# Attention and routed experts on one core: the hand-made list order is extended over the whole program, and the rows of a token tile are turned by transposes into one bank

## The chip, the cores and the metric

One core of a Trainium2 chip runs the whole program. The metric is device microseconds of one execution, median of three. The engines are PE (TensorE matmuls; PEld are its weight loads), DVE (VectorE), ACT (ScalarE), POOL (GpSimd) and SP (SyncE, which issues most DMAs). Each of them works through a queue in the order in which the program wrote it.

## The reference, cut to what matters

Two batches of eight heads attend over 576 positions with a learned bias on the distance. The 1152 output rows of 512 numbers then go to one of eight experts each, the best by a linear gate; an expert takes at most 288 rows, in order of the tokens.

```python
scores = scale * q @ k.T + bias          # bias: a two-layer net of log distances
attn = exp(scores - max) / (sum + 1e-09)
x = (attn @ v) as [1152, 512]
logits = x @ w_gate;  expert = argmax(logits);  gate = softmax(logits)[expert]
row i is kept if fewer than 288 earlier rows chose its expert
h = relu(x_e @ w1[e]);  y = h @ w2[e];  out[i] = gate * y   (0 if not kept)
```

## The kernel before, in words

**Attention.** There are 40 units: 10 token tiles (five of each batch, four of 128 rows and one of 64) by four pairs of heads. Unit n passes through these tasks, named as in the list that orders them:

- ("S", n): scores on PE into the PSUM pool "s" (two buffers of two banks each, which a full unit fills both).
- ("L", n, i): on DVE, L218, bias added and the row extreme taken; the bias tile bt has come back from a round trip through DRAM.
- ("X", n, i): the exponential on ACT, L225.
- ("R", n) and ("T", n): transposes on PE, L233. R puts the last 64 columns into spare columns of the score banks of unit n+2; T fills pool "tt".
- ("C", n, i): copies out of PSUM, on ACT or DVE. ("C", n, 2), L265, copies what R wrote.
- ("V", n): the product with v on PE, L288, into the one bank "av".

The bias itself is made in 36 blocks in the first 100 us: hidden rows ("H"), a product on PE ("M"), a copy to the tile bo ("E", L160 and L162), a store to DRAM ("D", L168).

**A token tile** (after four units). ("A"): av is copied to xT. ("BM"), tile_b, L319: xT is multiplied by a constant idwg of identity and gate weights side by side, 144 columns for each of four blocks of 128, into the banks "pt" and "av". ("BC"), tile_c: the DVE divides by the sums, first the logits (L355), then the rows x (L361), in four steps of the list. ("BD"): x is stored to DRAM.

**Routing.** The tiles form three groups. ("GA"), ("GB"), ("GC") turn a group's logits into a key for each row. ("P", z), pick, chooses the expert of stream z with most rows; ("MT", z, j), match (L442), and ("FE", z), fetch (L452 and the indirect loads of L460), bring its rows into X.

**The plain stream.** Three blocks of expert work run without branches: z = 0 and 1 for up to 288 rows, z = 2 for 96. Each has eight chunks of weights (load "WL", L639; high part "WH" on ACT or DVE; low part "WO" on DVE or POOL), turned rows ("XM", L654), the first layer in eight parts of 12 matmuls ("FM", L674, then "FH" and "FL" out of the bank) and the second layer of 4 x 24 matmuls (L707). Block 2 has its own forms (L746, L752, L723). Further experts sit behind branches and do not run here.

**The order.** Until the last attention unit every instruction is placed by place_tasks. It holds a clock for each engine, takes the tasks that can start within 0.3 us of the earliest, and writes out the one of lowest rank:

```python
first = min(b[0] for b in best)
at, rank, name, e, chosen = min((b for b in best if b[0] <= first + 0.3), key=lambda b: (b[1], b[0]))
```

Ranks are in units: L has n + 0.1, group 1 has 35.4 to 35.6, P(1) 35.7, P(2) and MT(1) 36, BC of a tile its last unit + 4.3. A task may take a bank, and the next user of it waits until the tasks named with it are done. In this part the expert blocks have the single bank "pt", which the row work of a tile, the routing and the fetches use as well. The DVE instructions for one score reduction, two picks and eight matches are thus in one fixed row.

After the list comes a second part, from tile_a(1, 4) on. The banks of the attention are given back, seven banks "fps" are opened (rest_pools), and the rest of block 0 (step(0, 10) onward: its second layer), the last tile, block 1 and block 2 are written in order for PE, while the framework orders the other engines.

Of the kernel before, what the change touches and what calls it, by code (L numbers as in the profile page):

```python
# [28 lines left out]
def kernel(ctx: ExitStack, tc: tile.TileContext, cap, ins, out):  # L29
# [15 lines left out]
    att = ExitStack()  # L45
    big = att.enter_context(tc.tile_pool(name="big", bufs=2, space=PSUM))
# [6 lines left out]
    kraw_p = att.enter_context(tc.tile_pool(name="kraw", bufs=8))  # L53
    qp = att.enter_context(tc.tile_pool(name="qp", bufs=3))
    vp = att.enter_context(tc.tile_pool(name="vp", bufs=4))
    ep = att.enter_context(tc.tile_pool(name="ep", bufs=4))
    atp = att.enter_context(tc.tile_pool(name="atp", bufs=4))
    vrp = att.enter_context(tc.tile_pool(name="vrp", bufs=4))
    bp = att.enter_context(tc.tile_pool(name="bp", bufs=4))
# [233 lines left out]
    xTs = {}  # L293
    bpt = {}
# [13 lines left out]
    def tile_b(b, t):  # L308

        n = 128 if t < 4 else 64  # L310
        xT = xTs.pop((b, t))

        if "ps" in F:
            ps = [ffn_psum() for _ in range(2)]
        else:
            ps = [pst.tile([128, 512], F32, name="pt"), psm.tile([128, 4, 128], F32, name="av").rearrange("p a c -> p (a c)")]
# [3 lines left out]
        if t == 4:  # L320
            nc.tensor.matmul(ps[1][:64, 256:260], lhsT=ident[:, 64:128], rhs=sums_t[b, t][:, 0:4], start=True, stop=True)
        bpt[b, t] = ps

    def tile_c(b, t):
# [11 lines left out]
        x = xp.tile([128, DM], F32, name="x")  # L336
        sums = sums_t.pop((b, t))
        inv = sm.tile([128, H], F32, name="inv")
        if t < 4:
            nc.vector.tensor_scalar(inv, sums, 1e-9, None, op0=ALU.add)  # L340
        else:
            iv = inv.rearrange("p (a r) -> p r a", r=2)
            nc.vector.tensor_scalar(iv[:64, 0], sums[:64, 0:4], 1e-9, None, op0=ALU.add)
            nc.vector.tensor_scalar(iv[:64, 1], ps[1][:64, 256:260], 1e-9, None, op0=ALU.add)
        nc.vector.reciprocal(inv[:n], inv[:n])
        yield
        for what in range(2):
            if what:
                yield
            for z, (k0, k1) in enumerate(((0, 3), (3, 4))):  # L350
                v = ps[z][:n, 0:144 * (k1 - k0)].rearrange("p (k c) -> p k c", c=144)
                h0, h1 = 2 * k0, 2 * k1
                iv = inv[:n, h0:h1].rearrange("p (k r) -> p k r", r=2).unsqueeze(3)
                if what == 0:
                    nc.vector.tensor_tensor(lg[:n, i, h0:h1].rearrange("p (k r) e -> p k r e", r=2),  # L355
                                            v[:, :, 128:144].rearrange("p k (r e) -> p k r e", r=2),
                                            iv.to_broadcast([n, k1 - k0, 2, E]), op=ALU.mult)
                else:
                    if z:
                        yield  # L360
                    nc.vector.tensor_tensor(x[:n, D * h0:D * h1].rearrange("p (k r d) -> p k r d", r=2, d=D),  # L361
                                            v[:, :, 0:128].rearrange("p k (r d) -> p k r d", r=2),
                                            iv.to_broadcast([n, k1 - k0, 2, D]), op=ALU.mult)
        xs[b, t] = x
# [130 lines left out]
    idwg = const.tile([128, 4, 144], F32, name="idwg")  # L495
# [9 lines left out]

    def gate_const():
        nc.vector.tensor_copy(idwg[:, :, 0:128], ident.unsqueeze(1).to_broadcast([128, 4, 128]))
        nc.vector.tensor_copy(idwg[:, :, 128:144], wgt.rearrange("p (k c) -> p k c", k=4))
# [64 lines left out]
    def rest_list():  # L573
# [8 lines left out]
        nc.vector.tensor_tensor(sel8, sel8, bc(need), op=ALU.mult)  # L582
        nc.vector.reduce_sum(lstf[:, 2 * E:2 * E + 1], need, axis=AX.X)
# [3 lines left out]
        nc.vector.reduce_sum(lstf[:, E:2 * E], tmp8, axis=AX.X)  # L587
        nc.vector.tensor_copy(lst[:, 0:2 * E + 1], lstf[:1, 0:2 * E + 1])
# [8 lines left out]
    def ffn_pools():  # L597
# [9 lines left out]
        Y.append(w0.tile([128, DM], F32, name="y0"))  # L607
# [33 lines left out]
    def weights(z, c):  # L641

        weights_load(z, c)
        split_w(RAW[c % len(RAW)], wbuf(z, c), "ad")

    def ffn_psum():
        return F.get("ps", pst).tile([128, 512], F32, name="pt")
# [3 lines left out]
    def x_mm(x, k, nb):  # L651
        px = fps["x", k] = ffn_psum()
# [16 lines left out]
    def l1_mm(f, w):  # L669
        wh, wl = (u.rearrange("p (k c) -> p k c", k=4)[:, :, 128 * (f % 2):128 * (f % 2) + 128] for u in w)  # L670
        ph = fps["h", f] = ffn_psum()
# [16 lines left out]
    def rows_out(z, a, py):  # L688

        y = Y[F["n"] % len(Y)]  # L690
        F["n"] += 1
        nc.scalar.activation(y[:TB], py[:TB], AF.Copy, scale=SLT[z][:, a, 0:1])
        d = nc.gpsimd.indirect_dma_start(  # L693
            out=out, out_offset=bass.IndirectOffsetOnAxis(ap=SLI[z][:, a:a + 1], axis=0), in_=y[:TB], in_offset=None,
# [4 lines left out]
    def layer2(d, ws):  # L699
# [58 lines left out]
    def step(z, i):  # L758

        if i < 2:  # L760
            for k in range(2 * i, 2 * i + 2):
                x_parts(X[0], k, NB)
            if z and i:
                for a in range(NB):
                    layer2_out(0, a)
# [461 lines left out]
```

## Time and profile before

| | us |
|---|---|
| median of three runs | 324.32 (321.94 to 325.65) |
| the profiled execution | 323.12 |
| its span, first to last instruction | 321.3 |
| PE / DVE / ACT / POOL busy | 268.0 / 205.6 / 171.8 / 87.2 |
| mean granted clock of TensorE, as a share of 2.4 GHz | 0.930 |

Busy times of PE are modelled from starts and pipelined ends, so a stretch in which PE is busy can still run at half clock: the granted clock beside it says at which of the two levels. The profiled execution lies 1.8 us above its span and 1.2 us under the median.

### The profile page before, as it was taken

How to read it: one execution, taken by the hardware profiler on the slowest of the kernel's cores; microseconds unless marked ns; L12 is line 12 of the kernel's file. 1: busy time of each engine (PE TensorE's matmuls, PEld its weight loads, DVE VectorE, ACT ScalarE, POOL GpSimd, SP SyncE). 2: the span in 40 equal slices, each digit the busy share in tenths (PEclk: the TensorE clock that was granted, in tenths of full speed). 3: DMA queues.
4: the chain of work that ended last, by engine and by line, in shares of the span. 5: the costliest groups of instructions: out<-in, count | busy, mean ns of one | idle time of the engine just before them, and what ended most of it. 6: DMA issues, size and time to landing. Idle time of an engine off the chain costs nothing. (4 is left out here: it accounts for less than half of the span.)

```text
span 321.3 us, 7361 instructions
## 1 busy us (share of the span) xinstructions
PE 268.0 (83%) x2801; PEld 202.6 (63%) x2801; DVE 205.6 (64%) x568; ACT 171.8 (53%) x401; POOL 87.2 (27%) x83
## 2 busy tenths in 40 slices
PE   2974977898899898988895989998398869999890
PEld 1521535544455686866584768887287869999870
DVE  4894898598578666577773856856832597950110
ACT  4874677697486546655554473554301357841230
POOL 3794496387460200001252100010030120300031
PEclk9999899999999799999958999999755989999997
DMA  6989595884954732998799575200220599300020
GB/s 172 359 251 332 164 372 157 277 317 150 325 225 152 277 125 65 338 288 265 231 310 290 149 257 155 61 35 0 67 86 22 211 338 414 118 2 0 2 75 16
DMA packets 27628, 59.84 MB, mean 186 GB/s; under 512 B 3813, under 2 KB 5349, under 8 KB 27585
## 3 DMA queue, kind: packets, MB, share of 16 engines
q1 hardware_dynamic: 26688, 56.82, 52.5%
q0 software_dynamic: 896, 2.47, 2.7%
q8 instruction: 24, 0.39, 0.5%
q14 instruction: 20, 0.16, 0.1%
HBM read 42.57 MB, written 16.99 MB: 185 GB/s over the span
## 5 line engine op out<-in xcount | busy, mean ns | idle before, releaser
L218 DVE CUSTOM_DVE_ANT_0 ed<-s,bt 128x576 f32<-128x576 f32 x72 | 53.2, 753 | 30.3 <-PE s L233 15.2
L128 POOL TENSOR_SCALAR hid<-c_u,nbv 128x400 f32<-128x400 f32 (+17 forms) x42 | 59.0, 1417 | 29.3 <-PE tt L147 14.5
L225 ACT ACTIVATE ed<-ed,mn 128x576 f32<-128x576 f32 x72 | 55.8, 776 | 15.8 <-DVE mn L218 14.6
L201 PE MATMUL s<-kraw,q 64*128 64x288 f32 x256 | 46.5, 439 | 4.3 <-ACT rt L265 3.1
L288 PE MATMUL av<-at,vt 128*64 128x128 f32 (+1 forms) x576 | 45.4, 291 | 2.4 <-DVE x L361 1.6
L288 PEld LDWEIGHTS av<-at,vt 128*64 128x64 f32 x576 | 35.8, 149 | 9.1 <-issue 2.8
L201 PEld LDWEIGHTS s<-kraw,q 64*128 64x128 f32 x256 | 25.9, 190 | 17.2 <-ACT rt L265 4.6
L130 ACT ACTIVATE hid<-c_u,c_v 128x528 f32<-128x528 f32 (+17 forms) x52 | 31.4, 659 | 7.8 <-PE tt L147 4.1
L233 PE MATMUL tt<-c_ident,ed 64*128 64x64 f32 x576 | 27.9, 237 | 3.3 <-DVE bo L160 1.7
L265 ACT COPY rt<-s 128x64 f32<-128x64 f32 (+1 forms) x68 | 11.2, 212 | 36.0 <-DVE mn L218 27.2
L233 PEld LDWEIGHTS tt<-c_ident,ed 64*128 64x128 f32 x576 | 23.1, 147 | 10.9 <-issue 4.8
L247 ACT COPY at<-tt 128x512 f32<-128x512 f32 x44 | 24.1, 581 | 6.7 <-PE tt L233 3.9
L132 DVE TENSOR_SCALAR hid<-c_u,c_v 128x544 f32<-128x544 f32 (+17 forms) x50 | 25.1, 543 | 0.0
L90 ACT CAST wh<-raw 128x1024 fp32r<-128x1024 f32 x16 | 16.6, 1050 | 14.7 <-PE av L288 7.8
L417 POOL TENSOR_SCALAR tokv<-s 128x5 bf16<-128x5 f32 (+2 forms) x3 | 1.6, 549 | 78.1 <-DVE s L415 70.0
L674 PE MATMUL pt<-xh,wh 128*128 128x288 f32 x64 | 21.2, 332 | 1.5 <-DVE hl L681 1.0
L95 DVE TENSOR_TENSOR wl<-raw,wh 128x1024 fp32r<-128x1024 f32 x16 | 19.5, 1219 | 3.6 <-ACT wh L90 3.4
L147 PE MATMUL pt<-hid,c_w2bd 128*32 128x432 f32 (+12 forms) x152 | 17.1, 512 | 4.9 <-DVE bo L160 4.7
L160 DVE TENSOR_SCALAR bo<-pt,c_rv,corr 128x192 f32<-128x192 f32 (+31 forms) x32 | 17.1, 576 | 5.4 <-DMA bd<-bo 3.4
L674 PE MATMUL pt<-xl,wh 128*128 128x288 f32 x64 | 20.4, 318 | 0.0
L674 PE MATMUL pt<-xh,wl 128*128 128x288 f32 x64 | 20.0, 312 | 0.0
L707 PE MATMUL pt<-hh,wh 128*128 128x288 f32 x64 | 20.0, 312 | 0.0
(176 smaller groups left out, 511.9 us busy)
## 6 DMA issues: line engine op xcount, KB each, us to landing
bt<-bd SPq DMA_DIRECT2D x28, 576.0 KB, 4.9
raw<-in_w_dram SPq DMA_DIRECT2D x24, 512.0 KB, 7.3
bd<-bo SPq DMA_DIRECT2D x36, 295.5 KB, 4.0
vt<-in_v_dram SPq DMA_DIRECT2D x8, 320.0 KB, 5.4
kraw<-in_k_dram SPq DMA_DIRECT2D x8, 288.0 KB, 4.7
bt<-bd SPq DMA_DIRECT2D x8, 288.0 KB, 4.5
out_dram<-y SPq DMA_DIRECT2D x3, 768.0 KB, 8.5
q<-in_q_dram SPq DMA_DIRECT2D x8, 256.0 KB, 6.4
```

The costliest lines, as they stand in the source:

```text
L95: (nc.vector if eng[1] == "d" else nc.gpsimd).tensor_tensor(lo, raw, hi.bitcast(F32), op=ALU.subtract)
L128: nc.gpsimd.tensor_scalar(hid[:, :m], wu[:, :m], nbv[:, w:w + 1], None, op0=ALU.max)
L130: nc.scalar.activation(hid[:, :m], wu[:, :m], AF.Relu, bias=bvw[:, w:w + 1])
L132: nc.vector.tensor_scalar(hid[:, :m], wu[:, :m], bvw[:, w:w + 1], 0.0, op0=ALU.add, op1=ALU.max)
L201: nc.tensor.matmul(ps[i][:, r, :HALF], lhsT=q[p, hp], rhs=k[p, r * HALF:(r + 1) * HALF], start=True, stop=True, tile_position=(64 * i, 0))
L218: nc.vector.tensor_tensor_reduce(out=ed.rearrange("p (r j) -> p r j", r=2), in0=ps[:, :, :HALF], in1=bias.rearrange("p (r j) -> p r j", r= ...
L225: nc.scalar.activation(ed, ed, AF.Exp, scale=-1.0, bias=mns.pop((n, i)), accum_out=total)
L233: nc.tensor.transpose(out[r][:w], ed[p, o:o + w], ident[p, p], tile_position=(64 * r, 0))
L247: nc.scalar.copy(o, v)
L288: nc.tensor.matmul(o, lhsT=lh, rhs=rh, start=(j == 0), stop=(j == 4), tile_position=(0, r))
L674: nc.tensor.matmul(ph[:, :cap], lhsT=u[:, k], rhs=x[:, k], start=(k + z == 0), stop=(k == 3 and z == 2))
L707: nc.tensor.matmul(py[:, :cap], lhsT=w, rhs=hx, start=(f + i == 0), stop=(f == 7 and i == 2))
```

## The change

- The list covers everything up to the last scatter. The second part is gone. Tasks exist for the last tile, group 2, the list of remaining experts, all three blocks and every scatter. PSUM is not handed over; block 1 and block 2 take one bank of any of the pools pt, tt, s and av ("ANY"), so five banks in all. SBUF is handed over by a task ("late") after the last V.
- tile_b is split. tile_l ("BL") makes the logits alone into 64 columns of a bank, with the plain gate weights; tile_c ("BC") becomes one step with one product; tile_b ("BM") turns the rows by four transposes into one bank; tile_x ("BX") scales them with one instruction. The bank "av" is not used by them. idwg and the 0.9 us of its making go.
- The model of the list gets other numbers and rules: a bandwidth of 380 KB/us for loads, no latency between tasks of one engine, shorter times for several tasks. ("C", n, 2) now comes after the score reductions of unit n+2, with which it shares banks.
- At the start, loads of K, Q and V wait in the list for earlier transfers (stores of bias blocks, bias tiles).
- Ranks of P, MT(1), L and the tiles stay, BC's becomes lower by one.

```diff
-    def tile_b(b, t):
+    def tile_l(b, t, w="pt"):
...
+        ps = bpt[b, t] = ffn_psum(w)
+        for k in range(4):
+            nc.tensor.matmul(ps[:n, 16 * k:16 * k + 16], lhsT=xTs[b, t][:, k, :n], rhs=wgt[:, 16 * k:16 * k + 16], start=True, stop=True)
...
+    def tile_b(b, t, w="pt"):
...
         for k in range(4):
-            z, o = divmod(144 * k, 432)
-            nc.tensor.matmul(ps[z][:n, o:o + 144], lhsT=xT[:, k, :n], rhs=idwg[:, k], start=True, stop=True)
...
+            nc.tensor.transpose(ps[:n, 128 * k:128 * k + 128], xT[:, k, :n], ident)
...
+    def tile_x(b, t):
...
+        nc.vector.tensor_tensor(x[:n].rearrange("p (h d) -> p h d", d=D), ps[:n].rearrange("p (h d) -> p h d", d=D),
+                                invs.pop((b, t))[:n].unsqueeze(2).to_broadcast([n, H, D]), op=ALU.mult)
...
-                ready = max([ends[a] for a in after], default=0.0)
+                own = engines if len(engines) == 1 and engines != "s" else None
+                ready = max([begun[a[1]] if a[0] == "then" else ends[a] if begun[a, "on"] != own else begun[a] for a in after], default=0.0)
...
+            if kb:
+                moved = max(moved, at + us[e] + 1.0) + kb / 380.0
+                ends[name] = moved + 1.0
...
-            task(("VL", b, hp), "s", 0.45, (lambda b=b, hp=hp: dma_v(b, hp)), after=[slot(17) if b else slot(hp - 3)],
-                 rank=20.0 * b + hp - 1, takes=[("v", users)])
...
+            task(("VL", b, hp), "s", 0.45, (lambda b=b, hp=hp: dma_v(b, hp)), after=[slot(17) if b else slot(hp - 1) or then("B", 0, 4, 1)],
+                 rank=20.0 * b + hp - 1, takes=[("v", users)], kb=320)
...
-        task(("C", n, 2), "da", {"d": 0.3, "a": 0.5}, (lambda e, n=n: turned_rem(n, e)), after=[("R", n)], rank=n + LAG + 0.3, takes=[("rt", [("V", n)])])
+        task(("C", n, 2), "da", {"d": 0.28, "a": 0.25}, (lambda e, n=n: turned_rem(n, e)),
+             after=[("R", n)] + ([("L", n + LAG, i) for i in two(n + LAG)] if not last else []), rank=n + LAG + 0.3, takes=[("rt", [("V", n)])])
...
+        spare = ("pt",) if i < 8 else ("pt", "s", "tt")
+        task(("BL", b, t), "e", 0.4, (lambda w="pt", b=b, t=t: tile_l(b, t, w)), after=[("A", b, t), "wg"], rank=n + 1.1, takes=[(spare, [("BC", b, t)])])
+        task(("BC", b, t), "d", 0.7, (lambda b=b, t=t: tile_c(b, t)), after=[("BL", b, t)], rank=n + 1.3)
+        task(("BM", b, t), "e", 0.9, (lambda w="pt", b=b, t=t: tile_b(b, t, w)), after=[("BL", b, t)], rank=n + 1.2, takes=[(spare, [("BX", b, t)])])
+        task(("BX", b, t), "d", 0.85, (lambda b=b, t=t: tile_x(b, t)), after=[("BM", b, t), ("BC", b, t)], rank=n + 1.5, takes=[("x", [("BD", b, t)])])
...
+    task("late", "p", 0.6, late_pools, after=[("V", n) for n in range(NU - 4, NU)] + ["pools"], rank=40.0)
...
+            task(("WO", z, c), "pd", {"p": 2.4, "d": 1.16},
+                 (lambda e, z=z, c=c, raw=raw: split_lo(e, *wbuf(z, c), raw())), after=[("WH", z, c)], rank=r + 2.5)
...
+    ANY = ("pt", "tt", "s", "av")
+    for z in range(2):
+        pp = ("pt",) if z == 0 else ANY
+        for k in range(4):
+            task(("XM", z, k), "e", 0.35, (lambda w="pt", k=k: x_mm(X[0], k, NB, w)), after=[("FE", z), ("FM", 0, 7) if z else None, "late" if z else None],
+                 rank=(27.0, 43.5)[z] + 0.1 * k, takes=[(pp, [("XL", z, k)])])
...
+            task(("FM", z, f), "e", 1.65, (lambda w="pt", z=z, f=f: l1_mm(f, wbuf(z, f // 2), w)),
+                 after=[("XL", z, k) for k in range(4)] + [("WO", z, f // 2)], rank=(30.0 + 1.4 * f, 50.0 + f)[z],
+                 takes=[(pp, [("FL", z, f)])])
...
+                task(("Y", z, d, g), "e", 0.82, (lambda w="pt", z=z, d=d, g=g: l2_mm(d, [wbuf(z, c) for c in range(4, 8)], g, w)),
+                     after=[("FL", z, 2 * g + 1), ("FL", z, 2 * g), ("WO", z, 4 + g), ("Y", z, d, g - 1) if g else None],
+                     rank=(44.0, 60.0)[z] + d + 0.2 * g,
+                     takes=[(ANY if (z or d) else ("pt",), [("YC", z, d)])] if g == 0 else [])
```

## Rows read from the trace of the kernel before

**Rows 1.** Busy time of the engines, granted clock and DMA, by stretches

```profile
core 0: us, PE busy (x) PEld busy (x) DVE busy (x) ACT busy (x) POOL busy (x), PEclk, DMA share, GB/s
...
24.60:30.16 5.56, 1.24 (x6) 0.69 (x6) 2.17 (x6) 1.90 (x5) 3.39 (x4) 1.00 1.02 342
30.16:226.15 195.99, 174.13 (x2078) 124.51 (x2078) 142.37 (x403) 118.97 (x305) 53.51 (x47) 0.96 0.63 208
226.15:231.05 4.90, 0.00 (x1) 0.01 (x2) 4.76 (x20) 0.92 (x3) 0.00 (x0) 0.76 0.35 107
231.05:249.40 18.35, 16.56 (x148) 14.43 (x149) 6.23 (x22) 4.01 (x11) 3.47 (x4) 0.51 0.16 48
...
261.60:313.90 52.30, 51.17 (x366) 48.02 (x363) 23.79 (x58) 23.65 (x44) 7.52 (x10) 0.97 0.32 118
```

**Rows 2.** Who PE waited for, 200 to 262 us: total, times, longest

```profile
PE s L233 <- ACT ed L225: 4.9, 1, 4.9
PE pt L404 <- DVE oh L386: 2.7, 1, 2.7
```

**Rows 3.** DVE in order of time, 219 to 230 us: start, duration, idle before

```profile
219.01 0.17 DVE L540 TENSOR_TENSOR kept<-pt,rows 128x8 f32<-128x8 f32 x1 [2.00 <-PE pt L539]
...
220.23 0.75 DVE L218 CUSTOM_DVE_ANT_0 ed<-s,bt 128x576 f32<-128x576 f32 x1
...
226.96 2.46 DVE L442 TENSOR_SCALAR match<-iota,key,base 128x288 bf16<-128x288 f32 x7
229.34 0.74 DVE L218 CUSTOM_DVE_ANT_0 ed<-s,bt 128x576 f32<-128x576 f32 x1
```

**Rows 4.** The chain that ended last, in order of time

```profile
192.40 1.78 PE pt L674 x12
...
241.61 3.19 PE pt L674 x12
```

**Rows 5.** PE in order of time, 206 to 231 us

```profile
206.10 1.00 PE L319 MATMUL pt<-idwg,xT 128*128 128x144 f32 x6
...
224.89 1.00 PE L319 MATMUL pt<-idwg,xT 128*128 128x144 f32 x6 [0.60 <-DVE hl L681]
```

**Rows 6.** DVE in order of time, 24 to 30 us

```profile
24.59 0.76 DVE L218 CUSTOM_DVE_ANT_0 ed<-s,bt 128x576 f32<-128x576 f32 x1 [1.23 <-DMA bt<-bd]
...
29.43 1.08 DVE L160 TENSOR_SCALAR bo<-pt,c_rv,corr 128x96 f32<-128x96 f32 x2 [3.39 <-DMA bd<-bo]
```

**Rows 7.** DMA issues of 0 to 36 us: count, KB each, us to landing

```profile
vt<-in_v_dram SPq DMA_DIRECT2D x4, 320.0 KB, 6.5
```

**Rows 8.** PE in order of time, 271 us: the output of block 0 turned

```profile
270.89 1.47 PE L714 MATMUL pt<-c_ident,yt 128*96 128x128 f32 x12
```

**Rows 9.** DVE in order of time, 231 us: the rows of a tile scaled

```profile
231.40 0.55 DVE L361 TENSOR_TENSOR x<-pt,inv 128x384 f32<-128x384 f32 x1
...
231.94 0.28 DVE L361 TENSOR_TENSOR x<-av,inv 128x128 f32<-128x128 f32 x1
```

**Rows 10.** Who waited for whom, whole span: total, times, longest

```profile
PE s L201 <- ACT rt L265: 3.1, 4, 1.1
```

**Rows 11.** The same, waits of ACT

```profile
ACT rt L265 <- DVE mn L218: 27.2, 17, 4.0
```

**Rows 12.** The same, waits of DVE

```profile
DVE ed L218 <- ACT rt L265: 7.6, 17, 1.0
```

**Rows 13.** PE in order of time, 172 to 175 us: rows of block 0 turned

```profile
172.35 0.30 PE L654 MATMUL pt<-c_ident,xe 96*128 96x96 f32 x1 [2.08 <-DMA xe<-xd,sli]
174.16 0.42 PE L654 MATMUL pt<-c_ident,xe 96*128 96x96 f32 x1 [1.51 <-DMA xe<-xd,sli]
```

**Rows 14.** POOL in order of time, 215 and 261 us

```profile
215.73 0.20 POOL L417 TENSOR_SCALAR tokv<-s 128x3 bf16<-128x3 f32 x1 [31.91 <-DVE s L415]
...
261.29 1.23 POOL L417 TENSOR_SCALAR tokv<-s 128x2 bf16<-128x2 f32 x1 [8.02 <-DVE oh L386]
```

**Rows 15.** DVE in order of time, 261 us

```profile
261.24 1.23 DVE L95 TENSOR_TENSOR wl<-raw,wh 128x1024 fp32r<-128x1024 f32 x1
```

More of the change, by code (lines that the diff above doesn't have):

```diff
@@ L335, in tile_c @@
         lg = glg[g]
[L336 removed]
         sums = sums_t.pop((b, t))
[L338 removed]
+        inv = invs[b, t] = sm.tile([128, H], F32, name="inv")
         if t < 4:
@@ L606, in ffn_pools @@
             F[nm] = w0.tile([128, m, cap], F32R, name=nm)
-        Y.append(w0.tile([128, DM], F32, name="y0"))
+        Y.extend(w0.tile([128, DM], F32, name=f"y{k}") for k in range(3))
+        F["yt"] = w0.tile([128, 4, cap], F32, name="yt")
         F["n"] = 0
@@ L775, in small, with st_hi @@
[L775 to L792 removed]
+    def st_hi(q):
+        nc.scalar.copy(F["sh"][:, 2 * q:2 * q + 2], fps["st", q][:, 0:2 * TB].rearrange("p (f c) -> p f c", f=2))
@@ L808, in fetch2 @@
     def fetch2():
-        for j in range(8):
-            match(2, j, 0, TB)
         fetch(2, X[1], 8, 0, 1)
@@ L886, in place_tasks @@
             at, rank, name, e, chosen = min((b for b in best if b[0] <= first + 0.3), key=lambda b: (b[1], b[0]))
-            engines, us, fn, after, rank, takes, late = left.pop(name)
+            engines, us, fn, after, rank, takes, late, kb = left.pop(name)
             for pool, (pools, users) in zip(chosen, takes):
@@ L982 @@
-    for g in range(2):
-        n = 22.0 if g == 0 else 34.0
+        task(("A", b, t), "da", {"d": 0.62, "a": 0.52}, (lambda e, b=b, t=t: tile_a(b, t, e)), after=[("V", 4 * i + 3)], rank=n + 0.8, takes=[("xT", [("BM", b, t)])])
+        spare = ("pt",) if i < 8 else ("pt", "s", "tt")
+        task(("BL", b, t), "e", 0.4, (lambda w="pt", b=b, t=t: tile_l(b, t, w)), after=[("A", b, t), "wg"], rank=n + 1.1, takes=[(spare, [("BC", b, t)])])
+        task(("BC", b, t), "d", 0.7, (lambda b=b, t=t: tile_c(b, t)), after=[("BL", b, t)], rank=n + 1.3)
@@ L1017 @@
-    task("clear", "p", 1.0, lambda: nc.gpsimd.memset(X[0], 0.0), after=[("XM", k) for k in range(4)], rank=33.0)
     task(("FE", 1), "e", 2.0, fetch1, after=[("MT", 1, j) for j in range(8)] + ["clear"] + [("BD", 1, t) for t in range(3)],
          rank=38.0, takes=[("pt", [("FE", 1)])], late=6.0)
+    task(("FE", 2), "e", 0.8, fetch2, after=[("MT", 2, j) for j in range(8)] + ["late"] + [("BD", 1, t) for t in range(3)],
+         rank=42.0, takes=[("pt", [("FE", 2)])], late=4.0)
+    task("pools", "p", 1.4, ffn_pools, after=[("D", n) for n in range(36)] + [slot(18)], rank=20.0)
@@ L1021 @@
+    task(("OY", 2), "ad", {"a": 0.6, "d": 0.65}, lambda e: y_row(2, 0, e), after=[("Z", 3)], rank=70.0, takes=[("y", [("OS", 2)])])
+    task(("OS", 2), "p", 1.05, lambda: y_send(2, 0), after=[("OY", 2)], rank=70.0, late=2.0)
     place_tasks({"e": 5.0, "d": 4.6, "a": 4.6, "p": 5.5, "s": 4.5})
     man.close()
-    man.enter_context(tc.manual_schedule(engines={ET.PE}))
-    def run(gen):
-        for _ in gen or ():
-            pass
-    urgent = {tile_a, tile_b, tile_c, tile_d, group_a, group_b, group_c, rest_list, fetch2}
@@ L1055 @@
-    for i in range(8, 12):
-        then(step, 1, i)
-    for c in range(4, 8):
-        then(weights, 2, c)
-    for i in range(12, 14):
-        then(step, 1, i)
-    for i in range(5):
-        then(small, i)
-    then(small, 5)
-    then(step, 1, 14)
-    then(small, 6)
-    for f, a in later:
-        if f in urgent:
-            with tc.high_priority():
-                run(f(*a))
-        else:
-            f(*a)
-    man.close()
+    rest_pools()
     n_rest = nc.values_load(lst[0:1, 2 * E:2 * E + 1], min_val=0, max_val=E)
```

373 lines of the change are left out of this document (187 added, 186 removed).

## The prediction

> **What bounds the kernel now.** I read the table of stretches first, cut where PE's work visibly changes [rows 1]. PE is the engine with the most work nearly everywhere: 174.13 of 195.99 us in the long middle, 51.17 of 52.30 us at the end. The last stretch is therefore a stream of matmuls with nothing left to gain by order, 1.1 us. The losses stand elsewhere. From 24.60 to 30.16 us PE has 1.24 us of work and the DMA engines are full (share 1.02). From 226.15 to 231.05 us PE has none at all, while DVE is busy for 4.76 of 4.90 us. Then PE does 16.56 us of work in 18.35 us, but at a mean granted clock of 0.51, the lower of its two levels (1.2 GHz).
>
> What that clock costs is read from one piece of work at both levels, the twelve matmuls of an FM: 1.78 us against 3.19 us [rows 4]. At 1.78/3.19 = 0.56 the 16.56 us would be 9.2 us, so 7.3 us are lost to the clock. It fell in the stretch without PE work: 0.76 on average there, 0.51 behind it.
>
> The waits say who made PE stand [rows 2]: 4.9 us for an exponential of ACT, in one piece, and 2.7 us for the group 2 choice on DVE. Behind the 4.9 us stands DVE's row [rows 3]. The score reduction of unit 37 waits until 220.23 us behind a pick (which itself waited 2.00 us for PE's count), and that of unit 38 until 229.34 us behind the second pick, a weight split and 2.46 us of matches. Meanwhile PE has nothing else: the rows of tile (1, 3), multiplied at 224.89 us [rows 5], hold the bank pt until DVE reads them behind those reductions, and the next FM needs that bank.
>
> **The change part by part.** The sum is made against the profiled execution (323.12 us, 1.8 us over its span).
>
> *The start.* Four V loads of 320 KB [rows 7] are among what is moved behind the first bias tiles, 1280 KB, at the 342 GB/s of rows 1 some 3.7 us of DMA time. The first reduction waited 1.23 us for its bias tile, a bias copy 3.39 us for an earlier store [rows 6]. At best both waits go, 4.6 us. But V is needed at the next unit, and the DMA engines stay full there, so I take 2 us; at worst the V loads meet the stores of the following blocks, minus 1.
>
> *A tile's rows.* Before, PE needs 1.00 us for the six instructions into pt and about 0.25 us more for the two into av [rows 5]. Four transposes of 128 columns cost 4/12 of 1.47 us = 0.5 us [rows 8]. Eight instructions of the logits are new, with as many weight loads as before and 16 columns instead of 144; no row shows that shape. Between nothing and the full 1.25 us I take 0.8, nearer to the old product because its weight loads are the same. So 1.3 us against 1.25: nothing on PE, with -0.75 to +0.5 us a tile as ends, -7 to +5 us over ten. On DVE two instructions for x (0.55 and 0.28 us [rows 9]) become one, and the logits come ahead of them at a lower rank, so that group 1 need no longer stand behind the rows in DVE's queue and can begin earlier. The constant idwg is off the path.
>
> *The middle.* 195.99 - 174.13 = 21.9 us of idle PE, and a mean clock of 0.96, which is 8% of 196 us at half clock, 16 us, worth up to 7 us. The new list places copies of R's columns behind the reductions that share their banks. Now DVE waits for ACT there in 17 cases, 7.6 us [rows 12], and ACT for DVE in 17, 27.2 us [rows 11]. The first kind goes; the second becomes the rule, and score matmuls behind those copies, 3.1 us in 4 cases [rows 10], may come to wait in twice as many, plus 3 us. Of what is idle I take 4 us as gained, for a list whose times are nearer to the trace, with -4 and +10 as ends: the part has many reasons, and each new order makes some of its own.
>
> *The hole at 226 us.* Its worth is 4.9 + 7.3 = 12.2 us. What works for it: group 1 starts earlier; tile (1, 3) may take a bank of s or tt, so pt is free for FM(0, 6) and FM(0, 7) while DVE works through its row; and second-layer tasks of block 0 are in the list as fill. What works against it: the ranks are unchanged. P(1) 35.7, P(2) and MT(1) 36 still stand before the reductions of units 37 to 39. I take 8 of 12.2.
>
> *Group 2 and the end of the first layer.* PE stood 2.7 us for the choice, because weight splits went first on DVE, and the last stretch has a mean clock of 0.97: 6% of 52.3 us, 3.1 us at half level, worth 1.4 us. In the list the group has its own place and PE can be given second-layer matmuls instead. I take 3 of 4.1.
>
> *The plain stream.* PE's work is the same and it is saturated. Five banks instead of seven could cost a wait here and there: 0, with -1 to +2 as the cost. The 7.4 us from 313.90 us [rows 1] to the end of the span, with the last scatter, stay.
>
> *POOL.* Low parts of the weights may now go to POOL in this part too. One row shows what DVE does to POOL: a 0.20 us instruction took 1.23 us at 261.29 [rows 14], beside DVE's weight split at 261.24 us that lasted as long [rows 15]. The split itself took no harm. I price it at nothing, since POOL has 7.52 us of work in 52.30. The Trainium skill, "SBUF — State Buffer", section "Who interferes with whom", says that a DVE instruction with two SBUF inputs and a GpSimd instruction that reads SBUF exclude each other for the whole instruction. The trace agrees with it in that row; by the rule a POOL split would block the next DVE split in turn, and the sum would lose a few us of DVE time that PE does not wait for.
>
> Sum of gains: 2 + 0 + 4 + 8 + 3 + 0 = 17 us, 323.12 - 17 = 306.1 us. The median of the runs lies 1.2 us over this execution: 307.3, so 307 us.
>
> **The rivals.**
>
> *The hole stays.* DVE's row is ordered by the same ranks, so units 38 and 39 wait as before, PE stands and the clock falls. For it: the ranks. Against it: the bank that is no longer held, and the earlier group. The 8 us are missing, 315 us.
>
> *PE stands at the rows of block 1.* XM(1) has rank 43.5, before the second layer of block 0 (44), and the list counts 6 us for the indirect loads. The same loads for block 0 came so late that PE stood at the head of its queue for 2.08 and 1.51 us [rows 13]. In the old order the rows of block 1 were turned only after the second layer, without a wait. If PE stands as long here, 3.6 us, and does as much work at half clock after it, 0.44 x 3.6 = 1.6 us, 5.2 us are lost: 312 us.
>
> *Slower: score banks given free last by the copies of R.* A unit of four rows of heads needs both score buffers. If the copy behind the reduction is the last reader each time, PE's score matmuls wait for it. Now 4 waits make 3.1 us, 0.78 us each [rows 10]. In all 40 units that is 31 us, against a gain of 17: 323.1 + 31 - 3 - 17 = 334, with the median's offset 335 us. It decides from 17/0.78 = 22 more units with the wait. For it: ACT waits for the reductions already in 17 cases. Against it: only 4 of those reached PE, since other matmuls stood between.
>
> *Everything is gained.* Hole and clock go wholly, and the middle gives 8: 299 us.
>
> *The list does nothing new.* The end is saturated already, so listing it could be worth nothing; then only the start, the middle and part of the hole remain, which is the first rival's time.
>
> **How the numbers follow.** Forecast, 303 to 312 us: 0.46. The hole stays, 315: 0.22. PE stands at block 1, 312: 0.13. Everything gained, 299: 0.10. Slower, up to 335: 0.09. The terms' own ends (start -1 to 4.6, tile -5 to 7, middle -4 to 10, hole 0 to 12.2) add in part to each other, so the range reaches from 298, the best case, to 320, the hole kept with a bad middle; about 2 in 10 lie outside, mostly in the last rival. A measurement of this kernel tells 1%, 3.2 us, from no change. Faster than 321 us: nearly all of the first four cases but 0.08 for a kept hole with a middle that loses 4 us or more, so 0.83; within 1%, 0.08; slower 0.09.
>
> **What the changed profile would show.** The hole: no stretch of several us without PE work between the last score matmuls and the last V, and the clock at 1.0 there; the last FM of block 0 ends some 10 us earlier. The start: the first reduction near 22 to 23 us. A tile: transposes near 0.5 us, logits near 0.8 us, no wait of V for x. The end: PE busy for about the same 50 us, and the scatter 17 us earlier. I am wrong if PE still stands for the exponentials of the last units, if its waits for the copies of R grow beyond some 17 us, or if new waits for banks or indirect loads show in the second layer of block 0.

## The result, and the profile after the change

The changed kernel takes 314.21 us (313.1 to 315.29, four runs), the kernel before 323.31 us beside it: a ratio of 0.9711 with a 95% interval of 0.9636 to 0.9786, 9.1 us faster. The forecast was 307 us and a range of 298 to 320 us. The time lies in the range, but about half of the forecast gain is missing (9.1 us of 17), and the trace shows that the kernel had it in hand some 60 us before its end.

The stretches, as in [rows 1], cut where PE's work changes (the changed kernel's span is 313.0 us):

```profile
30.16:224.57 194.41, 176.07 (x2172) 131.62 (x2165) 139.18 (x434) 123.08 (x276) 64.76 (x55) 0.96 0.67 222
224.57:232.00 7.43, 7.43 (x50) 5.68 (x50) 2.16 (x6) 1.08 (x4) 2.28 (x4) 0.54 0.83 229
232.00:252.30 20.30, 17.50 (x186) 16.00 (x185) 14.40 (x35) 9.26 (x16) 6.01 (x3) 0.92 0.71 247
252.30:266.70 14.40, 14.36 (x98) 13.96 (x97) 13.59 (x22) 11.93 (x19) 12.11 (x11) 0.87 0.69 223
266.70:274.99 8.29, 0.00 (x1) 0.00 (x1) 7.91 (x19) 0.41 (x1) 4.58 (x2) 0.68 0.04 18
274.99:313.00 38.01, 30.45 (x204) 28.31 (x204) 7.33 (x13) 8.74 (x19) 3.68 (x4) 0.90 0.07 20
```

The hole at 226 us is gone: PE is busy from 224.57 to 232.00 us without a break, although at the lower of its two clock levels (0.54, near 1.2 GHz). What made the clock fall there without a hole is not shown: in the 4.57 us before, PE was busy for 4.01 us at full clock. A new hole of 8.29 us stands at 266.70 us, deep in the stream that had 1.1 us of idle PE before. PE has no work in it, and DVE is busy for 7.91 us.

Who PE waited for, the whole span (total, times, longest), beside [rows 2, 10]:

```profile
PE tt L667 <- DVE hl L674: 8.3, 1, 8.3
PE s L202 <- DVE rt L266: 5.7, 4, 2.3
...
PE pt L397 <- DVE oh L379: 2.8, 1, 2.8
```

The wait for the exponentials, 4.9 us before, is not among them. The wait for the group 2 choice (oh) is, at 2.8 instead of 2.7 us. What DVE did while PE stood is read from its instructions in order of time, as in [rows 3], here from the first L529 on and with the last three score reductions (L219, units 37 to 39):

```profile
208.67 0.17 DVE L529 TENSOR_TENSOR kept<-kept,etab 128x8 f32<-128x8 f32 x1
...
218.64 0.74 DVE L219 CUSTOM_DVE_ANT_0 ed<-s,bt 128x576 f32<-128x576 f32 x1
...
221.42 0.74 DVE L219 CUSTOM_DVE_ANT_0 ed<-s,bt 128x576 f32<-128x576 f32 x1
...
226.54 0.76 DVE L219 CUSTOM_DVE_ANT_0 ed<-s,bt 128x576 f32<-128x576 f32 x1 [1.29 <-PE s L234]
...
247.20 2.73 DVE L379 TENSOR_TENSOR oh<-m,s 128x16 bf16<-128x16 f32 x1
...
254.37 2.03 DVE L429 TENSOR_TENSOR acc<-acc,m 128x8 bf16<-128x8 bf16 x1
...
262.00 9.31 DVE L529 TENSOR_TENSOR kept<-kept,etab 128x8 f32<-128x8 f32 x1
...
274.48 0.45 DVE L674 SCALAR_TENSOR_TENSOR hl<-tt,hh 128x288 fp32r<-128x288 f32 x1
```

Read the second column. The same line L529, a step of the picks that the list of remaining experts uses too, with the same eight columns, takes 0.17 us at 208.67 us and 9.31 us at 262.00 us. Nothing precedes it as a wait: it counts as busy, so no view of waits shows it. PE's 8.3 us end with the hl at 274.48 us, which stands in DVE's queue behind that instruction and the 3 us of small ones after it. What lay beside it is in POOL's row for the same time, which answers to [rows 14]:

```profile
244.38 3.14 POOL L453 DMA_INDIRECT xe<-xd,sli  x1 [6.12 <-DVE xl L655]
247.54 2.35 POOL L617 TENSOR_TENSOR wl<-raw,wh 128x1024 fp32r<-128x1024 f32 x1
...
254.02 2.36 POOL L617 TENSOR_TENSOR wl<-raw,wh 128x1024 fp32r<-128x1024 f32 x1
...
261.90 9.38 POOL L617 TENSOR_TENSOR wl<-raw,wh 128x1024 fp32r<-128x1024 f32 x4
```

Each of the three stretched DVE instructions lies beside low parts (L617) on POOL and ends with them: 249.93 beside 249.89 us, 256.40 beside 256.38, 271.31 beside 271.28. (The first of them starts 0.34 us before the low part's record does, which is not explained here; what is read is the common end.)

The chain that ended last, for the twelve matmuls of an FM, as in [rows 4]:

```profile
217.42 1.88 PE pt L667 x12
...
252.28 2.88 PE av L667 x12
256.92 1.59 PE pt L667 x12
...
274.99 3.25 PE tt L667 x12
```

The FM after PE's 2.8 us wait and the one after its 8.3 us wait run at half clock (2.88 and 3.25 us), those between at 1.59 us. So the stall costs more than its own length. The last FM of block 0 begins at 217.42 us; before it began at 245.78 us.

### The profile page after: what moved, and what is told of

It reads as the page before. It is cut to its first block, busy times and chain, and to the rows that moved or that the text cites. A ratio compares the mean times of both kernels' runs of the same rounds, so it can differ in the third digit from the quotient of the medians.

```text
span 313.0 us, 7462 instructions
## 1 busy us (share of the span) xinstructions
PE 264.4 (84%) x2841; PEld 203.9 (65%) x2841; DVE 203.7 (65%) x565; ACT 174.7 (56%) x369; POOL 112.6 (36%) x96
## 4 chain that ended last, share of the span: by engine, by line
PE 41%; DVE 12%; DMA 6%; ACT 5%; issue 4%; POOL 1%; SPq 0%; POOLq 0%; DVEq 0%; ACTq 0%
PE av L289 7%; PE s L202 6%; PE pt L667 4%; DMA raw<-in_w_dram 4%; PE tt L234 4%; DVE kept L529 3%; PE s L708 3%; ACT ed L226 3%; PE tt L708 2%; PE tt L667 2%; DVE wl L617 2%; DMA bt<-bd 1%; PE pt L315 1%; PE s L210 1%; PE pt L708 1%
## 5 line engine op out<-in xcount | busy, mean ns | idle before, releaser
L129 POOL TENSOR_SCALAR hid<-c_u,nbv 128x352 f32<-128x352 f32 (+17 forms) x48 | 67.0, 1408 | 23.8 <-PE pt L148 12.5
L219 DVE CUSTOM_DVE_ANT_0 ed<-s,bt 128x576 f32<-128x576 f32 x72 | 52.3, 752 | 26.9 <-PE s L234 11.1
L131 ACT ACTIVATE hid<-c_u,c_v 128x320 f32<-128x320 f32 (+17 forms) x51 | 30.5, 654 | 5.3 <-DVE c_v L478 2.9
L133 DVE TENSOR_SCALAR hid<-c_u,c_v 128x528 f32<-128x528 f32 (+17 forms) x45 | 24.9, 581 | 2.7 <-PE tt L148 1.9
L617 POOL TENSOR_TENSOR wl<-raw,wh 128x1024 fp32r<-128x1024 f32 x9 | 21.2, 2373 | 14.0 <-PE pt L667 7.8
L148 PE MATMUL pt<-hid,c_w2bd 128*32 128x512 f32 (+12 forms) x152 | 18.9, 547 | 3.5 <-ACT bo L163 2.1
L453 POOL DMA_INDIRECT xe<-xd,sli x7 | 9.4, 1348 | 31.7 <-DVE sli L451 17.7
L692 POOL DMA_INDIRECT out_dram<-y,sli x7 | 7.9, 1126 | 33.8 <-ACT y L686 32.0
L617 DVE TENSOR_TENSOR wl<-raw,wh 128x1024 fp32r<-128x1024 f32 x15 | 18.1, 1217 | 0.7 <-ACT wh L612 0.5
L148 PE MATMUL tt<-hid,c_w2bd 128*32 128x512 f32 (+12 forms) x136 | 13.5, 481 | 3.1 <-DVE bo L161 1.5
L289 PE MATMUL av<-rt,vt 128*64 128x128 f32 (+1 forms) x144 | 15.6, 275 | 0.5 <-ACT rt L266 0.5
L210 PE MATMUL s<-kraw,q 128*128 128x288 f32 x32 | 11.0, 476 | 3.9 <-DVE mn L219 3.9
```

The source lines that it names most:

```text
L129: nc.gpsimd.tensor_scalar(hid[:, :m], wu[:, :m], nbv[:, w:w + 1], None, op0=ALU.max)
L131: nc.scalar.activation(hid[:, :m], wu[:, :m], AF.Relu, bias=bvw[:, w:w + 1])
L133: nc.vector.tensor_scalar(hid[:, :m], wu[:, :m], bvw[:, w:w + 1], 0.0, op0=ALU.add, op1=ALU.max)
L148: nc.tensor.matmul(ps[32 * c:32 * c + 32, lo:hi], lhsT=w2bd, rhs=hids[n, c][:, lo:hi], start=True, stop=True, tile_position=(0, 32 * c))
L219: nc.vector.tensor_tensor_reduce(out=ed.rearrange("p (r j) -> p r j", r=2), in0=ps[:, :, :HALF], in1=bias.rearrange("p (r j) -> p r j", r= ...
L289: nc.tensor.matmul(o, lhsT=lh, rhs=rh, start=(j == 0), stop=(j == 4), tile_position=(0, r))
```

## The experiments

### GpSimd's subtractions

The first theory: POOL and DVE shut each other out, and the 9 us that are missing go to POOL's low parts. The first run leaves the order of the list and puts the low parts of z = 1 and 2 on DVE.

```diff
-                  (lambda e, ...: split_lo(e, *wbuf(z, c), raw())), after=[("WH", z, c)], rank=r + 2.5)
+                  (lambda e, ...: split_lo("d" if z else e, *wbuf(z, c), raw())), after=[("WH", z, c)], rank=r + 2.5)
```

> The order of the list is unchanged; only the low parts of the weights of blocks 1 and 2 that the list gave to POOL (6 of 16) are executed by DVE at their places. Theory 1, POOL and DVE shut each other out: small DVE instructions of two SBUF inputs last 0.17 us again instead of 9.31, 2.73 and 2.03 us, PE's wait of 8.3 us shrinks to about 4 (four low parts of 1.22 us stand there instead) and its wait of 2.8 us for the choice of group 2 to under 2, the clock falls less: 303 to 309 us. Rival, the order of DVE's queue: the chain of the list of remaining experts stands ahead of the copies that PE waits for, whatever POOL does, and DVE gets 7 us more of work: 314 to 319 us.

303.9 us, a ratio of 0.9459 (0.9394 to 0.9524). The 8.3 us wait is gone, and L529 takes 0.17 us at 258.12 us, although DVE has the work that POOL had for z = 1 and 2. The second run also tells the list that DVE does it:

```diff
-            task(("WO", z, c), "pd", {"p": 2.4, "d": 1.16},
+            task(("WO", z, c), "pd" if z == 0 else "d", {"p": 2.4, "d": 1.16},
...
```

> The list may place low parts of blocks 1 and 2 on DVE alone, so it also reorders. Theory 1: as the first run, and PE's long wait goes since the list counts DVE's time: 299 to 306 us. Rival, order of DVE's queue: DVE becomes the longest row behind the attention (16 x 1.2 us of low parts), PE waits for low parts of block 1 instead: 312 to 318 us.

300.98 us, 0.9356 (0.9313 to 0.9398). It is the best version that computes everything, 13 us under the changed kernel. It is the base of the later runs, except the third, fourth and ninth, which stand on the changed kernel.

The third run is the rival: that the place of the rest list in DVE's queue is the fault, not the exclusion.

```diff
-    chain(("RL",), "d", [1.2, 1.0, 1.0], rest_list(), after=[("GC", 2), ("P", 2)], rank=47.0, ...)
+    chain(("RL",), "d", [1.2, 1.0, 1.0], rest_list(), after=[("GC", 2), ("P", 2), ("FL", 1, 7)], rank=62.0, ...)
```

> POOL keeps its six low parts; the chain of the list of remaining experts comes behind the first layer of block 1 instead of in it. Rival, order of DVE's queue: PE's wait of 8.3 us and the half clock behind it go, 302 to 306 us. Theory 1: the next DVE instruction with two SBUF inputs, a low part of its own, is shut out in its place and the copies behind it wait for it, so that a long DVE instruction of that kind is still there; half or less of the 12 us comes back, 306 to 314 us.

305.6 us, 0.9489 (0.9452 to 0.9525). By the number the rival holds. But the exclusion is still there, and the choice of group 2 (L379) is held for 2.73 us as before; DVE in order of time, and then POOL:

```profile
244.60 2.73 DVE L379 TENSOR_TENSOR oh<-m,s 128x16 bf16<-128x16 f32 x1
...
260.04 3.90 DVE L617 TENSOR_TENSOR wl<-raw,wh 128x1024 fp32r<-128x1024 f32 x2
...
264.24 3.05 DVE L617 TENSOR_TENSOR wl<-raw,wh 128x1024 fp32r<-128x1024 f32 x1
```

```profile
262.84 3.37 POOL L617 TENSOR_TENSOR wl<-raw,wh 128x1024 fp32r<-128x1024 f32 x1 [1.12 <-ACT wh L612]
```

Both engines lengthen, each in its turn: POOL's low part begins while DVE is in the second of two (which end at 263.94 us) and is done 2.27 us after their end, at 266.21, about its usual 2.36 us. DVE's next one begins at 264.24 us and is done 1.08 us after POOL's end; alone it takes 1.22 us. Here the exclusion only shuts out something that PE did not need at once. So both things are needed for the 8.3 us: an exclusion, and copies for PE queued behind its victim.

The three runs leave one doubt. They also change DVE's load or the order. The ninth run keeps both engines' order and POOL's time, and takes away what POOL reads. For z = 1 and 2 POOL writes zeros into the low part, in three instructions of about the same total time; the low parts of six chunks are thus left out.

```diff
     def split_lo(eng, hi, lo, raw):
+        if eng == "z":
+            nc.gpsimd.memset(lo.bitcast(F32), 0.0)
+            nc.gpsimd.memset(lo.bitcast(F32), 0.0)
+            nc.gpsimd.memset(lo[:, 0:320].bitcast(F32), 0.0)
+            return
...
+                  (... split_lo("z" if z and e == "p" else e, *wbuf(z, c), raw())), ...
```

> The order of the changed kernel (314.21 us) to the instruction. Where it has GpSimd subtract for groups 1 and 2, GpSimd now writes zeros into the same low part, by three instructions that together take about the 2.4 us of the one subtraction and read nothing. It leaves out these low parts of the weights. Theory (a GpSimd instruction that reads SBUF shuts out VectorE's instructions with two inputs there, and the reverse; GpSimd being late by 2.4 us is harmless): 300 to 305, as in the run with those subtractions on VectorE (303.9 us), with the 128x8 product that took 9.31 us back at 0.2 us while GpSimd is as busy as before. Rival (it is enough that GpSimd uses SBUF at all, or that its 2.4 us make PE wait for the low part): 311 to 316, with VectorE's instruction as long as GpSimd's writes beside it.

297.67 us, 0.9244 (0.9107 to 0.938), 16.5 us under the changed kernel; by the two ratios 4.7%, 15 us. That is below even the range of my theory. POOL is busy for 112.3 us in all, as in the changed kernel (112.6). DVE's three instructions, with two low parts between them and a cast behind them:

```profile
245.83 0.17 DVE L379 TENSOR_TENSOR oh<-m,s 128x16 bf16<-128x16 f32 x1
...
246.16 2.36 DVE L622 TENSOR_TENSOR wl<-raw,wh 128x1024 fp32r<-128x1024 f32 x2
...
250.45 0.17 DVE L429 TENSOR_TENSOR acc<-acc,m 128x8 bf16<-128x8 bf16 x1
...
256.20 0.17 DVE L529 TENSOR_TENSOR kept<-kept,etab 128x8 f32<-128x8 f32 x1
...
258.66 0.73 DVE L578 CAST lst<-lstf 1x17 int32<-1x17 f32 x1
```

POOL's zeros beside them:

```profile
246.14 0.97 POOL L618 MEMSET wl<- 128x1024 f32 x1
...
250.07 0.96 POOL L618 MEMSET wl<- 128x1024 f32 x1
...
258.41 0.96 POOL L619 MEMSET wl<- 128x1024 f32 x1
```

Of the three, only the second lies beside zeros being written, the other two a little ahead of them. The two low parts of 246.16 us lie beside zeros too and keep their 1.2 us each. One cast does not: 0.73 us where the changed kernel has 0.17, ending with the zeros at 259.37 us, and the product queued behind it is late with it (0.65 for 0.20 us). So writing is not free for every DVE instruction; here PE did not wait for it.

The stretches of the same kernel, first to be compared with 232.00:252.30 above:

```profile
232.00:252.30 20.30, 20.05 (x213) 18.76 (x210) 14.31 (x45) 13.10 (x22) 8.81 (x12) 1.00 0.70 237
252.30:275.00 22.70, 22.15 (x170) 22.01 (x170) 13.20 (x33) 11.14 (x19) 13.27 (x16) 1.00 0.32 126
```

PE is busy nearly throughout at full clock, with POOL busy for 22.1 us in the two stretches, 22.7 in the changed kernel. That settles it against POOL's load and its lateness: what does the harm is its subtraction beside DVE instructions with two inputs in SBUF. The zeros differ from it in that they read nothing, but they are also another kind of instruction, and these runs do not tell the two apart. The Trainium skill, "SBUF — State Buffer", section "Who interferes with whom", says just this, that such a DVE instruction contends with a GpSimd instruction that reads SBUF and not with one that only writes; the runs agree, 9.31 us beside reads, 0.17 us and low parts of 1.2 us beside writes.

The eighth run asks whether the three low parts that POOL keeps within the attention (z = 0) should go too.

```diff
-            task(("WO", z, c), "pd" if z == 0 else "d", {"p": 2.4, "d": 1.16},
+            task(("WO", z, c), "d", {"p": 2.4, "d": 1.16},
...
```

> Base as in the run with the list that knows it (300.98 us), and now every low part is on VectorE, those of group 0's weights too, so GpSimd subtracts nothing. If the exclusion of the two engines decides in the middle of the stream too, as it does behind it: 297 to 300. If VectorE's time is short there (each low part is 1.2 us of it, and up to sixteen go over): 302 to 306, with more waits of PE for reductions.

304.74 us, 0.951 (0.9448 to 0.9573), in the range of the second branch and 3.8 us above its base by the medians. But its four runs go from 300.07 to 307.65 us, and those of the base from 299.13 to 302.47, so the size is loose and the difference not quite sure. New among PE's waits are 4.0 us for hl. No gain from moving these three is seen; that DVE's time is short there fits, but the run doesn't show it by itself.

### The parts of the change

The fourth run, on the changed kernel, undoes the start: the loads of K, Q and V wait for the slots they had before.

```diff
-after=[slot(n0 - 8), then("B", 0, 4, 1)]
+after=[slot(n0 - 8)]
...
-after=[then("D", hp - 1)],
...
-after=[slot(17) if b else slot(hp - 1) or then("B", 0, 4, 1)]
+after=[slot(17) if b else slot(hp - 3)]
```

> The conditions on the first loads of K, Q and V are those of before; all else is the changed kernel. Theory: the moved K loads stand among the stores of the bias blocks and make the first bias tile late (first reduction at 26.1 us, before 24.6); with them undone it starts near 24.6 us again and the end comes 1 to 2 us earlier, 312 to 313 us. Rival: the loads then compete with the following stores, as before, and the time at the end of the bias part is the same, 314 to 315 us.

315.23 us, 0.9761 (0.9708 to 0.9813): no measurable difference from the changed kernel at the end. On the way there is one. The 65th of the 72 score reductions, one of the last tile but one, comes 1.9 us later than in the changed kernel (194.74 us), and later than in the traces of the first three, the seventh and the ninth run, which have the new start and much the same order up to there (193.3 to 194.7). It is weak evidence, as the tenth run's long execution, with the new start too, has 199.1 us:

```profile
196.59 0.75 DVE L219 CUSTOM_DVE_ANT_0 ed<-s,bt 128x576 f32<-128x576 f32 x1
```

At the first FM of block 1 the two are level again (252.21 and 252.08 us): the changed kernel has by then run its 7.4 us at half clock, while this run's clock is 0.85 from 226 to 235 us. The first reduction waits longer for its bias tile after the change than before [rows 6], not shorter:

```profile
26.13 0.76 DVE L219 CUSTOM_DVE_ANT_0 ed<-s,bt 128x576 f32<-128x576 f32 x1 [4.23 <-DMA bt<-bd]
```

It comes at 25.37 us with the old start, and with the new one at 24.60 and 24.90 us in the first two runs, so it varies by most of the 2 us that I had counted on.

The fifth run brings back the old rows of a tile on the base of the second: 144 columns into pt and av, four steps on DVE, and V waits for the tile before.

```diff
+            nc.tensor.matmul(ps[z][:n, o:o + 144], lhsT=xT[:, k, :n], rhs=idwg[:, k], start=True, stop=True)
...
+        task(("BM", b, t), "e", 1.2, (lambda b=b, t=t: tile_b(b, t)), after=[("A", b, t), "gate"], rank=n + 1.2,
+             takes=[("pt", [("BC", b, t)]), ("av", [("BC", b, t)])])
+        chain(("BC", b, t), "d", [0.5, 0.5, 0.6, 0.4], tile_c(b, t), after=[("BM", b, t)], rank=n + 2.3, ...)
```

> The low parts of group 1's weights stay on VectorE in the planner's choice too, as in the run with the list that knows it (300.98 us), and the rows of a tile are made as before the change: the product with the 144-column matrix into a pt bank and the av bank, four steps on VectorE, and V of a unit waits for the tile before it. Theory (taking the rows out of av and splitting logits from rows is worth something, because V no longer stands behind four VectorE steps): 303 to 306, with waits of PE for the reductions' or tile's VectorE steps back in the middle. Rival (the new rows cost PE 0.35 us a tile, eight logit matmuls of 1.0 us and four transposes of 0.59 us against 1.25 us, and buy nothing): 298 to 301.

313.42 us, 0.9771 (0.9713 to 0.9829): 12 us over its base, more than twice what either theory allowed. The loss is not spread over the tiles. The 65th score reduction comes at 199.2 us (194.6 in the base), the last at 242.4 us (227.0): 4.6 us are lost up to the ninth of the ten tiles, 10.8 us behind it. PE in order of time shows where: the list runs FMs of block 0 through the one bank pt, and the last scores come after them.

```profile
222.55 0.40 PE L678 MATMUL pt<-xh,wh 128*128 128x288 f32 x1 [4.00 <-DVE hl L685]
...
240.02 1.24 PE L210 MATMUL s<-kraw,q 128*128 128x288 f32 x4
```

The new rows thus pay most where the last tiles and block 0 want the same bank. As the whole list moves with them, I can't say how much of the 12 us is the bank av and how much pt.

The sixth run lifts the rule that copies of R's columns (rt in the traces, "the routing row" in the expectation) come after the reductions of unit n+2.

```diff
-             after=[("R", n)] + ([("L", n + LAG, i) for i in two(n + LAG)] if not last else []), rank=n + LAG + 0.3, ...)
+             after=[("R", n)], rank=n + LAG + 0.3, ...)
```

> Base as in the run with the list that knows it (300.98 us). The copy of the routing row (C of unit n) may be placed ahead of the reductions of the unit two further on. Theory (the late copies cost PE: its score matmuls wait 5.7 us for the routing row, against 3.1 us in the kernel before): 297 to 300, and that wait falls to 3 us or less. Rival (VectorE then waits for ScalarE in the place of PE, as it did before with 17 waits, and the reductions come later): 302 to 305.

314.84 us, 0.9745 (0.9678 to 0.9813), 14 us over its base. PE's waits for rt do fall, to 2.7 us in 3 cases, as the theory had it; yet the time goes the other way and far beyond the rival. PE's waits for mn on DVE are 9.9 us instead of 3.0. Two stretches show the rest:

```profile
50.00:62.00 12.00, 10.22 (x82) 6.33 (x82) 6.38 (x18) 6.28 (x16) 3.92 (x5) 0.57 0.52 169
...
215.00:235.00 20.00, 15.79 (x173) 12.85 (x172) 12.29 (x52) 6.22 (x19) 2.95 (x3) 0.68 0.18 59
```

The clock is 0.57 in the first and 0.68 in the second (0.89 and 0.91 in the base), and PE idles for 1.8 and 4.2 us. At the prediction's 0.44 us for each us at half clock I estimate 4.5 and 5.6 us for the clock, so the half clock beside these stalls cost more than the stalls.

The seventh run gives the last four units' reductions a rank ahead of picks and matches.

```diff
-rank=n + 0.1 + 0.01 * i
+rank=min(n, 35.0) + 0.1 + 0.01 * i
```

> Base as in the run with the list that knows it (300.98 us). The reductions of the last four units of the stream get a rank ahead of the picks and matches of block 0 that stand between them. Theory (the last scores stage ends later than it need, and the half clock after 225 us is the rest of the hole): 296 to 299, with the last scores matmul ahead of its place. Rival (the group chain of block 0 comes later by as much, and the first expert tokens with it): 300 to 303.

301.25 us, 0.9371 (0.9313 to 0.943), the same as its base. The last reduction comes 14 us earlier, and PE's clock falls all the same behind it:

```profile
212.79 0.75 DVE L219 CUSTOM_DVE_ANT_0 ed<-s,bt 128x576 f32<-128x576 f32 x1
```

```profile
225.00:235.00 10.00, 9.29 (x85) 8.23 (x84) 3.15 (x14) 1.00 (x3) 3.48 (x4) 0.55 0.67 218
```

My theory that the last reductions still hold up the end falls: in this order they are no longer on the path.

The tenth run leaves the second layer and blocks 1 and 2 the banks of pt and tt alone.

```diff
-    ANY = ("pt", "tt", "s", "av")
+    ANY = ("pt", "tt")
```

> Base as in the run with the list that knows it (300.98 us). The second layer of block 0 and blocks 1 and 2 may take banks of pt and tt alone, two instead of five. Theory (a bank is held for its matmuls of 1.6 us and some 0.8 us of copies, so two banks nearly keep PE supplied in the plain stream, but the tail's small steps stall): 305 to 310, and PE waits for copies of the first layer in more cases. Rival (five banks give nothing over two): 300 to 303.

322.11 us, 0.9873 (0.9639 to 1.0106): my 305 to 310 us was far too low. Its runs go from 315.75 to 326.64 us; by the two ratios it is some 17 us over its base, with a wide interval. The trace is of the slowest of them and is read with that in mind: the 65th reduction, ahead of the banks in question, is already 4.5 us later than in the base, the first FM of block 1 is 20.6 us later (267.44 against 246.86 us). In between the clock is 0.68 from 215 to 252 us, and from 252 us on PE waits for one bank after the other, some 9 us in all up to 285 us. The longest of these waits:

```profile
275.16 0.51 PE L667 MATMUL tt<-xh,wh 128*128 128x288 f32 x1 [2.43 <-DVE y L688]
```

The eleventh run lets the list count a latency between tasks of one engine again.

```diff
-                own = engines if len(engines) == 1 and engines != "s" else None
+                own = 0
```

> Base as in the run with the list that knows it (300.98 us). The model of the list counts a latency between two tasks of one engine again, as before the change. Theory (part of what the middle gained, 201.4 to 194.7 us at the 65th score reduction, comes from a model nearer to the trace): 303 to 308, with that reduction at 197 us or later. Rival (the model's latencies change little that PE sees): 299 to 302, the reduction at 194 to 196 us.

321.32 us, 0.9963 (0.9907 to 1.0019), 20 us over its base, far outside both ranges and as slow as the kernel before. The other numbers of the list were left as the change has them, so it is no pure undoing. In the trace, of an execution of 327.49 us, the 65th reduction comes at 229.1 us, since the list now places much of block 0 ahead of the last tiles. PE in order of time has two of the new waits:

```profile
54.29 1.51 PE L148 MATMUL pt<-hid,c_w2bd 128*32 128x384 f32 x8 [4.61 <-DVE bo L161]
...
281.83 0.91 PE L445 MATMUL pt<-tokv,match 128*96 128x6 bf16 x8 [5.07 <-DVE hl L674]
```

## Why the prediction came out as it did

Three marks divide the gain: the 65th score reduction (201.4 us before, 194.7 after, 193.3 in the ninth run), the first FM of block 1 (272.33, 252.08, 247.36) and the end of the span (321.3, 313.0, 296.6). Gains in us:

| stretch, terms | forecast | the change | ninth run (POOL reads nothing there) |
|---|---|---|---|
| to the 65th reduction: start, tiles, middle | 6 | 6.7 | 8.1 |
| to the first FM of block 1: hole, group 2 | 11 | 13.6 | 16.9 |
| to the end: plain stream, POOL | 0 | -11.9 | -0.3 |
| sum | 17 | 8.3 | 24.7 |

*The step that failed* is the term "POOL", priced at nothing. At 252 us the changed kernel was 20.2 us ahead, more than the whole forecast; 11.9 us went back behind that point, 16.4 us against the ninth run's end. I had the row [rows 14] and the rule, and then let POOL's load (7.52 us in the old last stretch) decide. Two things were missed. The change gives POOL up to four low parts in a row, and the shut-out lasts for the row, not for one instruction. And I named DVE time "that PE does not wait for", without asking what stands behind the blocked instruction in DVE's queue: the hl that frees PE's next bank. None of the signs of being wrong that I had listed looks there, in the first layer of block 1.

*The start* (2) and *the middle* (4) together fit, 6.7 us measured to the 65th reduction. By the fourth run's trace, one execution, the start is 1.9 us of it and the rest, 4.8 us, that of the middle and the tiles. The sign I had named for the start, a first reduction near 22 to 23 us, did not come (26.13), and at the end its gain is no longer there.

*A tile's rows.* Logits cost PE 0.99 us until V begins, not 0.8; transposes are as estimated (0.49 us until the scores behind them begin), and the one step for x on DVE takes 0.69 us where two took 0.83. PE and then DVE in order of time, beside [rows 5, 9]:

```profile
199.07 1.07 PE L315 MATMUL pt<-wgt,xT 128*128 128x16 f32 x8
200.06 1.09 PE L289 MATMUL av<-at,vt 128*64 128x128 f32 x16
...
201.31 0.66 PE L325 MATMUL pt<-c_ident,xT 128*128 128x128 f32 x4
```

```profile
202.00 0.69 DVE L356 TENSOR_TENSOR x<-pt,inv 128x512 f32<-128x512 f32 x1
```

So the term "nothing on PE" is about right, 0.2 us a tile more than before, and yet by the fifth run the part is worth some 12 us, most of it at the end of the attention, which I had put, unpriced, among the reasons for the hole.

*Copies of R.* "Plus 3 us" for PE's waits: 3.1 us became 5.7 for DVE and 0.7 for ACT. The slower rival needed 22 more units with the wait; there is one more. The sixth run shows that the rule which makes these waits saves far more than they cost in this list.

*The hole.* PE's scores of units 37 and 38:

```profile
205.13 1.22 PE L210 MATMUL s<-kraw,q 128*128 128x288 f32 x4
...
208.29 1.22 PE L210 MATMUL s<-kraw,q 128*128 128x288 f32 x4
```

Their reductions come some 12 us after them, at 218.64 and 221.42 us (unit 38's was at 229.34 us before [rows 3]), behind both picks and the matches. So DVE's row did stay as the ranks order it, as the rival "the hole stays" said. But PE no longer stands meanwhile: from 203.4 to 218.6 us it is busy for 13.77 of 15.2 us at full clock, with FMs and the second layer of block 0. In that the rival fell, although the measured time is nearly its 315 us. What I expected, full clock there, came only in part: 7.4 us at 0.54. With the second stretch of the table the term was too small, 13.6 to 16.9 us against 11, and the tenth run points to what carries it, block 0's second layer and block 1 as fill in five banks: some 16 us of its loss lie in that stretch, waits and half clock together.

*Group 2.* Its wait stayed, 2.8 us for 2.7, but for another reason: not a weight split in DVE's queue but a 0.17 us instruction held for 2.73 us beside POOL. Without that (ninth run) PE waits 0.25 us there.

*PE stands at the rows of block 1*: fell. PE's waits for indirect loads [rows 13] are gone at block 0 as well; the longest left there is 0.78 us, for DVE (L647 at 163.22 us).

*The list does nothing new*: the time is again nearly its own, 314 for 315 us, but it fell. In the ninth run the second stretch gains 16.9 us, more than the whole worth of the hole and group 2 (12.2 + 4.1 us), which is all that this rival had to give there. The eleventh run is no test of it, as it orders the whole list anew; it shows that one rule of the list's model, with the change's other numbers, is worth 20 us.

So the time fell into the range by luck, through two errors of opposite sign: the term for the hole and group 2 was too small by 2.6 to 5.9 us, that for POOL by 11.9 to 16.4 us.

## What to carry to other kernels

When work moves to GpSimd, count it as VectorE time too where both read SBUF and VectorE's instructions have two inputs there, and look first for what waits in VectorE's queue behind the instruction that may be shut out. In a trace, compare the duration of the same small instruction at different places: a long one is no wait in any list, and a lengthened 0.17 us instruction is how an exclusion looks. A gain that is reached in mid-kernel can be lost after it, so mark two or three points of the work and compare the lead at each.

## What the runs showed of the hardware

The shut-out goes on over several instructions in a row, with no place taken between them: 9.31 us on DVE beside four of POOL, and 9.33 us in the fourth run. It goes the other way too, as the low part on POOL in the third run shows (3.37 us). In the fifth run an indirect gather on POOL took 9.35 us (0.96 to 1.36 us elsewhere in it) while DVE worked through a row of low parts; POOL, then DVE:

```profile
256.46 9.35 POOL L459 DMA_INDIRECT xe<-xd,sli  x1 [6.33 <-DVE sli L457]
```

```profile
255.68 5.75 DVE L628 TENSOR_TENSOR wl<-raw,wh 128x1024 fp32r<-128x1024 f32 x5
...
262.02 2.35 DVE L628 TENSOR_TENSOR wl<-raw,wh 128x1024 fp32r<-128x1024 f32 x2
```

The gather of 3.14 us at 244.38 us in the changed kernel, beside two low parts on DVE, is the same in small, and it is there in the ninth run as well (3.14 us at 243.00). DVE's two subtractions were not lengthened by it (2.35 us from 244.32 us). This gather ends 0.85 us after them (247.52 and 246.67 us), and so it is in the first to fourth and the ninth run, 0.84 or 0.85 us each. In the fifth it ends 0.85 us after a cast that stands behind the low parts (264.96 us). That fits a gather held until DVE's row is done; it was not tried by itself.
